# New planner constants for the head of an mLSTM and two-MLP kernel: filling matmuls, sigmoids, ranks

## The chip, the core and the metric

The kernel runs on one core of a Trainium2 chip. The metric is the device time of one execution in microseconds (us); the median of three timed runs stands for a kernel. Engines are TensorE (PE; its weight loads are PEld), VectorE (DVE), ScalarE (ACT), GpSimd (POOL) and SyncE (SP), which here only issues DMAs.

## What is computed

An mLSTM over 4 batches of 8 heads with 768 steps of dimension 40, and then two dense blocks on 3072 tokens with 320 features and 2048 hidden ones. Cut to what matters:

```python
m_new = maximum(f_gate[t] + m, i_gate[t])
f_stab, i_stab = exp(f_gate[t] + m - m_new), exp(i_gate[t] - m_new)
C = f_stab * C + i_stab * outer(v[t], k[t])
n = f_stab * n + i_stab * k[t]
y[t] = sigmoid(o_gate[t]) * (C @ q[t]) / maximum(abs(n @ q[t]), 1)
# first dense block            second dense block
h = x @ w_in                   h = x @ w_in
g = 0 | (h+1)**2/4 | h         g = maximum(h, 0)**2
x = g @ w_out                  out = g @ w_out
```

In the first dense block g is 0 for h <= -1, h for h >= 1 and the parabola between.

## The kernel before

**Tiling.** The sequence is cut into 24 chunks of 128 steps (4 batches of 6); a chunk is also a tile of 128 tokens. The order of the chunks is the first chunk of each batch, then the second of each, and so on. In this text "the first, second, third chunk" are the first chunks of batches 0, 1 and 2, and the fourth is that of batch 3.

**The gates** (`gate_part`, L380) are handled in two parts: part 0 is the first chunk of each batch, part 1 is the other five. Each runs a scan (L388), subtractions (L394 to L399), three exponentials on ACT (L405, L408, L411), some memsets and a copy on DVE (L414 to L416) and a scan (L419); the input gates are transposed by PE (L443) and copied by ACT (L447).

**Attention** (`attention`, L457) of a chunk: `spread` (L507) puts the decays of four heads on all partitions with PE, twice a chunk; `decay` (L512) is a DVE scan over them; `last` (L518) copies their last column with ACT; `scores` (L540) is PE; `weigh` (L521) multiplies the scores by the decays on DVE; `v_in`, `k_in` and `q_in` (L547, L569, L561) are POOL or DVE; `outer` (L575) makes the new state with PE, `update` (L585, L589) adds it; `read` (L612, L616) gives the output, which is normed (L626 to L631, L636) with the sigmoid `sig` (L553) of the output gate. `again` (L641) copies 64 columns. `to_xT` (L655, L665) transposes it with PE and splits it in a high and a low part, for dense products in two parts.

**Weights** (`weights`, L280). There are 16 blocks of 128 hidden features for each dense block. One comes as 64-bit floats by one DMA (L286); ACT (L290) and DVE (L298, L299, L303, L311) turn it into a 32-bit float, a copy gives the high part `w` (L272), and a subtraction the low part (L320, L324 on DVE or POOL). For the blocks listed in PLO the low part is made by PE instead (`plo`: L352, L353, in two halves, each copied out by ACT), one half after the other in the order of the block's number; these halves use the PSUM bank `acc2`.

**Dense** (`dense`, L676). Three chunks make a token block; for a token block j and a feature block f, `mm1` (L697) gives the hidden features, ACT, DVE and POOL apply the gate and split it, `mm2` (L750) adds to the output in `acc0` to `acc2`. The first three token blocks take feature blocks 0 to 7 in turn and then 8 to 15.

**What sets the order.** `Plan.order` (L58) is a list scheduler. Each step has a rank, the engines it can run on, a planned duration, and what it needs and makes. Whenever an engine is free in planned time, the ready step with the lowest rank is taken; steps that share the SBUF port of DVE and POOL exclude each other in the plan; buffers of a tag are handed out by the rank of the step that allocates. The list it gives is the order in which each engine runs its instructions on the chip, with no change at run time. Ranks are set as follows: chunk number m has a rank `at` from AT, or later from its token block's first use minus LEAD1; a weight block has WAT (first dense block), and its DMA's rank is lower by WDMA; the gates' part 1 has GATE, and its two stores to DRAM GATE + GDMA; a sigmoid has `at - 4`, plus SIGL for the first two chunks.

**Filling matmuls** (L815, L818). FILL matmuls of 128x128 by 128x160 bf16, which compute nothing that is used, have a rank behind all else, so that they go wherever PE has nothing ready in planned time. The planned duration is 0.22 for the first 30 and FDUR for the others.

```python
for i in range(FILL):
    plan.add(T, -97 if i == 0 else 1e6, 0.22 if i < 30 else FDUR, lambda i=i: idle(i == 0), ...)
...
plan.add(A, at - 4 + SIGL * (c == 0 and b < 2), act(DM), sig, [("vko", n)], [("sg", n)])
...
plan.add(Y, rank - WDMA, 2.75, load, make=[("wraw", K)])
```

Of the kernel before, what the change touches and what calls it, by code (L numbers as in the profile page):

```python
# [35 lines left out]
class Plan:  # L36
# [3 lines left out]

    TABLE = {"sig": "sigmoid", "a1": "exp", "a2": "exp", "a3": "exp"}
    LAT = {"T": 0.25, "SP": 1.9}

# [12 lines left out]
    def order(self):  # L58
        n = len(self.steps)
        maker, inst, users, alloc = {}, {}, {}, {}  # L60
        for i, (eng, rank, fn, need, make) in enumerate(self.steps):
            for key in make:
                assert key not in maker, key
                maker[key] = i
                if key[:2] not in alloc:
                    alloc[key[:2]] = i
                    inst.setdefault(key[0], []).append(key[1])
            for key in need + make:
                users.setdefault(key[:2], set()).add(i)
        deps = [set() for _ in range(n)]  # L70
        for i, (eng, rank, fn, need, make) in enumerate(self.steps):
            deps[i] |= {maker[key] for key in need}
        for tag, seq in inst.items():
            if tag not in self.bufs:
                continue
            b = self.bufs[tag]
            seq.sort(key=lambda x: self.steps[alloc[tag, x]][1])
            for k in range(1, len(seq)):
                if alloc[tag, seq[k]] != alloc[tag, seq[k - 1]]:
                    deps[alloc[tag, seq[k]]].add(alloc[tag, seq[k - 1]])  # L80
                if k >= b:
                    deps[alloc[tag, seq[k]]] |= users[tag, seq[k - b]]
        left = [len(d) for d in deps]
        after = [[] for _ in range(n)]
        for i, d in enumerate(deps):
            assert i not in d, self.steps[i]
            for j in d:
                after[j].append(i)
        ready, on = [0.0] * n, [None] * n
        free, queue = {}, {}  # L90

        def enqueue(i):
            rank, options = self.steps[i][1], self.steps[i][0]
            best = None
            for e, dur in options.items():
                q = queue.setdefault(e, [])
                ahead = sum(self.steps[k][0][e] for k in q if self.steps[k][1] <= rank)
                end = max(free.setdefault(e, 0.0) + ahead, ready[i]) + dur + (PEN if best else 0)
                if best is None or end < best[0]:
                    best = end, e  # L100
            on[i] = best[1]
            queue[best[1]].append(i)

        for i in range(n):
            if not left[i]:
                enqueue(i)
        out = []
        port, table = 0.0, None
        while len(out) < n:
            t, eng = min((max(free[e], min(ready[i] for i in q)), e) for e, q in queue.items() if q)  # L110
            i = min((i for i in queue[eng] if ready[i] <= t), key=lambda i: (self.steps[i][1], i))
            queue[eng].remove(i)
            out.append((t, i))
            dur = self.steps[i][0][eng]
            want = self.TABLE.get(self.steps[i][2].__name__)
            if want and want != table:
                table, dur = want, dur + 1.3
            shared = eng == "P" or isinstance(dur, Shared)
            free[eng] = end = (max(t, port) if shared else t) + dur
            if shared:  # L120
                port = end
            for j in after[i]:
                left[j] -= 1
                lat = 0.02 if eng in self.steps[j][0] and eng != "SP" else self.LAT.get(eng, 0.1)
                ready[j] = max(ready[j], end + lat)
                if not left[j]:
                    enqueue(j)
        self.span = max(free.values())
        return [(self.steps[i][2], on[i]) for _, i in out]
# [17 lines left out]
def act(n):  # L147
    return 0.2 + n * 0.00084
# [10 lines left out]
TURNS1 = [(0, 0, 8), (1, 0, 8), (2, 0, 8), (0, 8, 16), (1, 8, 16), (2, 8, 16)]  # L159
TURNS2 = [(6, 0, 8), (7, 0, 8), (6, 8, 16), (7, 8, 16), (8, 0, 8), (9, 0, 8), (8, 8, 16), (9, 8, 16)]  # L160
SPR = 6
AT = [-24, -19, -12, -4, 2, 2.0, 5.5, 8.5, 10.0]
WAT = [-13, -13.0, -7.5, -7.5, -3, -3.5, 1, 0.0, 6.0, 14.5, 16.0, 17.5, 16.5, 23.0, 22.5, 28.0]
LEAD1 = {3: [10.0, 11.5, 3.5], 4: [10.5, 6, 2.0], 5: [11.0, 8.0, 4.5], 6: [11.5, 7.5, 7.5], 7: [9.0, 5, 4.0]}
LEAD2 = {3: [12, 9, 3], 4: [12, 9, 6, 3]}
XTB, PAB = 3, 9
RAWB, DB = 3, 2
EARLY = 1
QB = 1
GATE = -14  # L170
FILL, FDUR = 140, 0.2
SIGL, GDMA = 3, 6
PLO = (0, 2, 3, 5, 6, 7)
WLEAD2 = (13, 0)
WDMA = 6
SGNV, LOV = (4, 4), (4, 0)
GLOV = (0, 1, 2, 3)

# [6 lines left out]
def kernel(  # L185
# [81 lines left out]
    def av(n):  # L267
        return {A: act(n), V: dve2(n)}
# [11 lines left out]
    def weights(part, f, rank):  # L280
# [46 lines left out]
        sg = P if f % 4 >= SGNV[part] else V  # L327
        plan.add(Y, rank - WDMA, 2.75, load, make=[("wraw", K)])
        plan.add(A, rank, act(WH), a_abs, [("wraw", K)], [("wt", K)])
# [8 lines left out]
        plan.add(av(WH), rank, 0, a_hi, [("wt", K, 3)], [(W, part + 1)])  # L338
        if part == 0 and f in PLO:
            plo(f, rank, z)  # L340
# [6 lines left out]
    def plo(f, rank, z):  # L347
        W, K = f"w{f}", (0, f)
        for i, (c0, c1) in enumerate(((0, WH // 2), (WH // 2, WH))):
            def sub(c0=c0, c1=c1):  # L350
                x = t_["idle_ps"][:, 0:c1 - c0]
                nc.tensor.matmul(out=x, lhsT=ident, rhs=z["t"][:, c0:c1], start=True, stop=False)  # L352
                nc.tensor.matmul(out=x, lhsT=nident, rhs=z["w"][:, c0:c1], start=False, stop=True)  # L353

            def put(c0=c0, c1=c1):
                x, w = t_["idle_ps"], z["w"]
                copy(A, w[:, WH + c0:WH + min(c1, WL)], x[:, 0:min(c1, WL) - c0])
                if c1 > WL:
                    copy(A, w[64:128, WL:c1], x[64:128, WL - c0:c1 - c0])

            key = ("acc2", -1, f, i)
            last = plan.plo
            plan.plo = key + (1,)
            plan.add(T, rank, 0.85, sub, [("wt", K, 3), (W, 1), ("acc2", -1), ("nid", 0), last], [key])
            plan.add(A, rank, act(352) + 0.2 * i, put, [key], [key + (1,), (W, 1, 1 + i)])
# [464 lines left out]
    gate_part(0, 1, -50)  # L830
    gate_part(1, NCB, GATE)
    for f in range(NF):
        weights(0, f, WAT[f])
    m = 0
    for j, (part, mine) in enumerate(blocks):
        nch = len(mine)
        for k, n in enumerate(mine):
            if part == 0:
                at = first_of[j] - LEAD1[j][k] if m >= len(AT) else AT[m]
                m += 1  # L840
# [6 lines left out]
    for f in range(NF):  # L847
        weights(1, f, max(last_of[0, f] + 1, first_use[1, f] - WLEAD2[f // 8]))
    for j, f0, f1 in visits:
# [84 lines left out]
```

## Time and profile before

| | |
|---|---|
| Median of three timed runs | 888.95 us (888.65 to 889.16) |
| The profiled execution | 887.01 us |
| its span on the core | 885.2 us |
| PE busy | 868.0 us |
| DVE busy | 468.3 us |
| ACT busy | 443.5 us |
| POOL busy | 333.1 us |

A row of the timeline gives the start and the duration in us, the engine, the line of the kernel, the operation, what it writes and reads, and how many instructions are merged in it; the bracket is the idle time of the engine just before it and what ended it. The windows give busy time of each engine in a stretch, and as PEclk the granted share of TensorE's full clock (1.00 is 2.4 GHz, 0.50 is 1.2 GHz). The ends of matmuls are modelled, so pieces of PE overlap a little.

### The profile page before, as it was taken

Reading aid. Unit: us, or ns where it says so; the run is one execution under the profiler, and the core shown is the slowest. Engines: PE = TensorE matmul, PEld = TensorE weight load, DVE = VectorE, ACT = ScalarE, POOL = GpSimd, SP = SyncE. Lnnn points to the kernel's source line nnn. Section 1 sums busy time; section 2 is a strip of 40 time slices with the busy share of each in tenths; the row PEclk is TensorE's granted clock in tenths of the full one; section 3 lists DMA queues with packets and bytes.
Section 4 is the critical chain, followed back from the end, with each engine's and each line's share of the span. In section 5 each row is a group of like instructions: output and inputs, shape, how many; then the busy total and the mean of one; then the engine's idle time right before and its main releaser. Section 6 shows DMA issues by size and latency. Waiting matters only on the chain.

```text
span 885.2 us, 14965 instructions
## 1 busy us (share of the span) xinstructions
PE 868.0 (98%) x5782; PEld 845.9 (96%) x5782; DVE 468.3 (53%) x834; ACT 443.5 (50%) x919; POOL 333.1 (38%) x318
## 2 busy tenths in 40 slices
PE   7989999999999999999999999999999999999997
PEld 6868999999999999999999999999999999999997
DVE  4788888996765655345437788822222222222221
ACT  5255457764554554545568765533343434343433
POOL 3212431003221246446335666533333333333333
PEclk6789999999999999999999999999999999999999
DMA  6555562455441434334002333011010000000000
GB/s 202 186 180 163 172 176 88 142 171 165 124 125 47 120 106 122 108 100 124 28 10 68 131 121 126 10 34 41 26 33 26 25 26 16 8 16 9 16 9 23
DMA packets 55979, 75.72 MB, mean 86 GB/s; under 512 B 7252, under 2 KB 44792, under 8 KB 55908
## 3 DMA queue, kind: packets, MB, share of 16 engines
q1 hardware_dynamic: 55908, 74.77, 27.1%
q8 instruction: 45, 0.74, 0.3%
q14 instruction: 26, 0.21, 0.1%
HBM read 65.90 MB, written 8.85 MB: 84 GB/s over the span
## 4 chain that ended last, share of the span: by engine, by line
PE 93%; DVE 3%; DMA 2%; ACT 1%; issue 0%; SPq 0%; DVEq 0%; ACTq 0%
PE h L697 39%; PE acc L750 38%; PE v L616 4%; PE s L540 3%; PE s L655 2%; PE v L612 2%; PE v L575 1%; PE s L507 1%; PE acc L352 1%; DMA vko<-in_vko_dram 1%; DVE d L512 1%; DVE wt L303 1%; DMA qk<-in_qk_dram 0%; PE acc L818 0%; PE h L507 0%
## 5 line engine op out<-in xcount | busy, mean ns | idle before, releaser
L750 PE MATMUL acc<-w,g 128*128 128x320 f32 x2304 | 379.3, 311 | 0.0
L750 PEld LDWEIGHTS acc<-w,g 128*128 128x128 f32 x2304 | 350.6, 188 | 2.5 <-DVE o L778 0.3
L697 PE MATMUL h<-xTh,w 128*128 128x384 f32 x1280 | 351.8, 340 | 0.4 <-DVE r L715 0.3
L725 POOL TENSOR_TENSOR g<-r,g 128x384 fp32r<-128x384 f32 x192 | 204.9, 1069 | 285.0 <-ACT g L272 270.1
L697 PE MATMUL h<-xTl,w 128*128 128x384 f32 x768 | 258.8, 337 | 0.0
L697 PEld LDWEIGHTS h<-xTh,w 128*128 128x128 f32 x1280 | 233.4, 188 | 1.7 <-DVE r L715 0.9
L717 DVE TENSOR_TENSOR r<-r,h 128x384 f32<-128x384 f32 x128 | 70.8, 554 | 233.4 <-ACT r L704 233.3
L272 ACT ACTIVATE g<-r 128x384 fp32r<-128x384 f32 x256 | 133.5, 523 | 114.2 <-DVE r L717 64.3
L697 PEld LDWEIGHTS h<-xTl,w 128*128 128x128 f32 x768 | 144.8, 189 | 0.0
L704 ACT ACTIVATE r<-h 128x384 f32<-128x384 f32 x128 | 62.7, 490 | 137.3 <-PE h L697 104.6
L702 ACT ACTIVATE r<-h,half 128x384 f32<-128x384 f32 x128 | 74.1, 579 | 94.1 <-PE h L697 91.6
L715 DVE SCALAR_TENSOR_TENSOR r<-r,h 128x384 f32<-128x384 f32 x128 | 70.0, 548 | 72.6 <-ACT r L708 69.4
L708 ACT ACTIVATE r<-r 128x384 f32<-128x384 f32 x128 | 67.0, 523 | 3.0
L512 DVE TENSOR_TENSOR_SCAN d<-fb,csb 128x512 f32<-128x512 f32 x36 | 50.2, 1395 | 9.5 <-PE v L616 9.4
L547 POOL TENSOR_TENSOR vt<-vko,it 128x369 f32<-128x369 f32 x24 | 23.1, 961 | 80.0 <-PE v L616 53.6
L616 PEld LDWEIGHTS v<-vt,d 128*128 128x128 f32 x384 | 49.1, 197 | 0.5
L616 PE MATMUL v<-vt,d 128*128 128x41 f32 x384 | 49.2, 279 | 0.0
L569 POOL TENSOR_TENSOR kt<-vko,ws 128x360 f32<-128x360 f32 x19 | 16.8, 885 | 75.2 <-ACT ws L518 75.2
L725 DVE TENSOR_TENSOR g<-r,g 128x384 fp32r<-128x384 f32 x64 | 37.9, 594 | 8.7 <-ACT g L272 8.3
L521 DVE TENSOR_TENSOR d<-s,d 128x512 f32<-128x512 f32 x48 | 31.5, 680 | 17.8 <-PE s L540 17.6
L561 POOL TENSOR_TENSOR qt<-qh,ab 120x384 f32<-120x384 f32 x20 | 22.2, 1110 | 35.6 <-DMA ab<-a 28.3
L595 POOL TENSOR_TENSOR C<-cx,csb 120x369 f32<-120x369 f32 x16 | 15.4, 960 | 53.3 <-DVE cx L589 50.2
(76 smaller groups left out, 686.7 us busy)
## 6 DMA issues: line engine op xcount, KB each, us to landing
wraw<-in_wts_dram SPq DMA_DIRECT2D x32, 704.0 KB
vko<-in_vko_dram SPq DMA_DIRECT2D x24, 524.5 KB
fb<-f SPq DMA_DIRECT2D x18, 512.0 KB
qk<-in_qk_dram SPq DMA_DIRECT2D x48, 160.0 KB
x<-x SPq DMA_DIRECT2D x24, 192.0 KB
x<-o SPq DMA_DIRECT2D x24, 160.0 KB
out_dram<-o SPq DMA_DIRECT2D x24, 160.0 KB
qh<-in_qh_dram SPq DMA_DIRECT2D x20, 180.0 KB
```

Of the source, the lines that this page charges most:

```text
L272: nc.scalar.activation(out=out, in_=in_, func=ACTF.Copy)
L512: nc.vector.tensor_tensor_scan(out=d.rearrange("p h t -> p (h t)"), data0=(z["fb"][a] if spr else z["fb"][:, 4 * a:4 * a + 4]).rearrange(" ...
L521: nc.vector.tensor_mul(out=z["d", a], in0=z["s", a], in1=z["d", a])
L616: nc.tensor.matmul(out=z["y"][:, E * h:E * (h + 1)], lhsT=z["d", a][:, h - 4 * a], rhs=z["vt"][:, h], start=(h == 0 and c == 0), stop=True ...
L697: nc.tensor.matmul(out=h, lhsT=a, rhs=b, start=(i == 0), stop=(i == 7))
L702: nc.scalar.activation(out=r, in_=z["h"], func=ACTF.Relu, scale=0.5, bias=half)
L704: nc.scalar.activation(out=r, in_=z["h"], func=ACTF.Relu)
L708: nc.scalar.activation(out=z["r"], in_=z["r"], func=ACTF.Square)
L715: nc.vector.scalar_tensor_tensor(out=r, in0=r, scalar=1.0, in1=z["h"], op0=ALU.min, op1=ALU.max)
L717: nc.vector.tensor_mul(out=r, in0=r, in1=z["h"])
L725: engine[e].tensor_sub(out=z["g1"], in0=z["r"], in1=z["g0"].bitcast(F32))
L750: nc.tensor.matmul(out=acc[k][:, 0:DM], lhsT=a, rhs=b, start=(f == f0 and i == 0), stop=(f == f1 - 1 and i == 2))
```

## The change

All constants below feed the planner; the steps and their instructions stay as they are, except that the low parts of feature blocks 1 and 4 of the first dense block are made by PE and ACT instead of DVE or POOL. There are 170 filling matmuls instead of 140, with a planned duration of 0.135 instead of 0.2 for those behind the thirtieth. Steps of PE that start before 5 us of planned time are planned at twice their duration. The two first sigmoids have ranks higher by 6. The ranks of chunks and weights, the gates' part 1, its stores and the weight DMAs are set anew.

```diff
+    COLD = 5.0
     TABLE = {"sig": "sigmoid", "a1": "exp", "a2": "exp", "a3": "exp"}
...
+            if eng == "T" and t < self.COLD:
+                dur *= 2
...
-AT = [-24, -19, -12, -4, 2, 2.0, 5.5, 8.5, 10.0]
-WAT = [-13, -13.0, -7.5, -7.5, -3, -3.5, 1, 0.0, 6.0, 14.5, 16.0, 17.5, 16.5, 23.0, 22.5, 28.0]
-LEAD1 = {3: [10.0, 11.5, 3.5], 4: [10.5, 6, 2.0], 5: [11.0, 8.0, 4.5], 6: [11.5, 7.5, 7.5], 7: [9.0, 5, 4.0]}
+AT = [-24, -19, -13, -4, 1.5, 2.0, 5.5, 8.5, 13.0]
+WAT = [-13, -10.0, -7.5, -7.5, -3, -6.5, 1, 0.0, 12.0, 15.0, 17.5, 17.5, 15.5, 22.0, 22.5, 25.5]
+LEAD1 = {3: [11.0, 12.0, 3.0], 4: [12.5, 8, 2.0], 5: [9.0, 5.0, 2.5], 6: [14.5, 10.5, 10.5], 7: [9.5, 5.5, 4.5]}
...
-GATE = -14
-FILL, FDUR = 140, 0.2
-SIGL, GDMA = 3, 6
-PLO = (0, 2, 3, 5, 6, 7)
-WLEAD2 = (13, 0)
-WDMA = 6
+GATE = -13
+FILL, FDUR = 170, 0.135
+SIGL = 9
+GDMA = 13
+PLO = (0, 1, 2, 3, 4, 5, 6, 7)
+WLEAD2 = (13, -1)
+WDMA = 7
```

## Rows read from the trace of the kernel before

**Rows 1.** The page, busy us of each engine, share of the span, instructions.
```profile
PE 868.0 (98%) x5782; PEld 845.9 (96%) x5782; DVE 468.3 (53%) x834; ACT 443.5 (50%) x919; POOL 333.1 (38%) x318
```

**Rows 2.** Windows: start:end, length, busy of PE, PEld, DVE, ACT, POOL; PEclk, DMA, GB/s.
```profile
30.00:35.00 5.00, 5.00 (x38) 4.46 (x37) 2.76 (x7) 0.00 (x0) 2.23 (x3) 0.50 0.08 25
35.00:40.00 5.00, 4.73 (x35) 3.86 (x33) 4.97 (x8) 2.44 (x6) 1.00 (x1) 1.00 0.75 247
40.00:45.00 5.00, 3.10 (x36) 2.79 (x34) 4.83 (x12) 2.26 (x4) 1.66 (x2) 1.00 0.77 259
45.00:50.00 5.00, 4.96 (x24) 4.06 (x24) 4.54 (x7) 2.97 (x6) 0.38 (x1) 0.52 0.29 82
...
60.00:70.00 10.00, 8.71 (x56) 6.86 (x57) 9.83 (x15) 7.50 (x18) 0.79 (x1) 1.00 0.42 147
...
80.00:90.00 10.00, 10.00 (x62) 8.18 (x61) 8.42 (x19) 4.70 (x12) 3.73 (x4) 0.86 0.65 213
```

**Rows 3.** Timeline of PE, 13 to 67 us.
```profile
13.07 0.72 PE L818 MATMUL acc<-x 128*128 128x160 bf16 x4
...
17.98 2.32 PE L818 MATMUL acc<-x 128*128 128x160 bf16 x16
21.17 2.04 PE L507 MATMUL s<-w,csb 36*128 36x128 f32 x8 [0.88 <-DVE d L521]
...
32.61 2.53 PE L818 MATMUL acc<-x 128*128 128x160 bf16 x18
35.41 0.53 PE L655 MATMUL s<-csb,xn 128*128 128x128 f32 x3 [0.27 <-DVE xn L636]
...
50.77 1.75 PE L540 MATMUL s<-qk 40*128 40x128 f32 x16
...
66.55 0.44 PE L697 MATMUL h<-xTh,w 128*128 128x384 f32 x1
```

**Rows 4.** Timeline of DVE, 19 to 65 us.
```profile
19.39 0.59 DVE L415 MEMSET w<- 36x640 f32 x1
20.02 0.42 DVE L416 COPY w<-w 36x5 f32<-36x5 f32 x1
...
43.10 0.29 DVE L320 TENSOR_TENSOR w<-wt,w 64x128 fp32r<-64x128 f32 x1
43.40 1.18 DVE L324 TENSOR_TENSOR w<-wt,w 128x576 fp32r<-128x576 f32 x1
...
48.01 1.22 DVE L512 TENSOR_TENSOR_SCAN d<-s,csb 128x512 f32<-128x512 f32 x1 [0.43 <-PE s L507]
...
52.55 1.29 DVE L521 TENSOR_TENSOR d<-s,d 128x512 f32<-128x512 f32 x2 [2.07 <-PE s L540]
...
61.97 0.51 DVE L298 TENSOR_SCALAR wt<-wt 128x704 f32<-128x704 f32 x1
62.51 0.53 DVE L299 TENSOR_SCALAR wt<-wt 128x704 int32<-128x704 int32 x1
...
64.19 0.53 DVE L665 TENSOR_TENSOR xTl<-s,xTh 128x384 fp32r<-128x384 f32 x1
```

**Rows 5.** Timeline of ACT, 8 to 18 us.
```profile
8.15 1.28 ACT L553 ACT_TABLE_LOAD   x1
10.46 0.47 ACT L553 ACTIVATE sg<-vko 128x320 f32<-128x320 f32 x1 [1.02 <-DMA vko<-in_vko_dram]
...
17.09 0.21 ACT L518 ACTIVATE ws<-d 128x4 f32<-128x4 f32 x1 [0.27 <-DVE d L512]
```

**Rows 6.** Timeline of PE, one half of a low part at full clock.
```profile
56.84 0.80 PE L352 MATMUL acc<-wt,csb 128*128 128x352 f32 x2
57.20 0.59 PE L353 MATMUL acc<-w,nident 128*128 128x352 f32 x1
57.63 0.31 PE L818 MATMUL acc<-x 128*128 128x160 bf16 x2
```

**Rows 7.** Waits of PE behind 66 us: us in total, times, longest.
```profile
PE v L612 <- DVE cx L589: 1.4, 2, 1.0
```

## The prediction

> **What bounds the kernel now.** I read the busy shares first: TensorE (PE) is busy for 98% of the span [rows 1], and every window behind 130 us shows it full. The page's shares hide the head, so the next view is the table by windows [rows 2]. There the reader sees three things. PE is "busy" in 30:35 at half clock (1.2 GHz), and what it does is partly filling matmuls that compute nothing. In 40:45 it is busy for only 3.10 of 5 us, and in 45:50 the clock is back at half. And VectorE (DVE), which is busy for only 2.76 of 5 us in 30:35, is full from 35 us on (4.83 of 5, then 9.83 of 10 in 60:70). The timeline of PE [rows 3] gives the date that counts: the first dense matmul (L697, feature block 0 of token block 0) starts at 66.55 us. From there on PE hardly waits any more; the largest wait listed is 1.4 us in two pieces [rows 7]. So the end is that date plus PE work that the change hardly touches: **a microsecond off the head is a microsecond off the kernel**, as long as PE stays full behind it.
>
> What holds 66.55? The first dense matmul needs three chunks through attention and transposed; the last step of that is the low half of the third chunk's transpose on DVE, at 64.19 us [rows 4]. Going back from it on DVE from 64 to 35 us nothing is idle but two waits, both for PE: 0.43 us before a decay scan (L512) and 2.07 us before the third chunk's weighing (L521) [rows 4]. So the head is, from 35 us on, DVE's work plus 2.50 us. Before 35 us it is PE at half clock: spreads (L507) of 2.04 us each, outer products, reads, scores, one behind the other [rows 3].
>
> **How the planner's edits become an order.** All ranks, FILL, FDUR and COLD only feed a list scheduler; on the chip each engine runs its queue in that fixed order. I use its planned times for one thing, who stands before whom and how many fills go into a gap (planned gap divided by the planned length of a fill); no duration is taken from it.
>
> **Fills.** A fill at half clock takes 2.32/16 = 0.145 us [rows 3]. FDUR goes from 0.2 to 0.135, near the cold one, so a planned gap gets half as many again. COLD doubles the first ones' planned length up to 5 us of planned time: 19 instead of 30 stand before the first transpose. PE waits there for the gates anyway, so that costs nothing. Along the cold stretch:
> - before the first spread 4 fills become 6: 2 x 0.145 = +0.29. PE waits for nothing there, so this is on the path.
> - before the first spread of the second chunk there are 16, a planned gap of 3.2 us, and PE then still waits 0.88 us for DVE [rows 3]. DVE is late there because the memset and copy of the later gates (0.59 and 0.42) stand before the weighing [rows 4]. In the changed plan the second chunk's sigmoid no longer holds ACT, the first chunk's `last` copies are planned 1.3 us earlier, and the weighing is picked first. The planned gap falls to 2.4 us, so 18 fills. DVE releases about 1.0 us earlier, but 18 x 0.145 = 2.6 us of fills behind a spread that ends 0.3 later let PE go at about 20.9 instead of 21.17: -0.27.
> - before the reads 2 become 4: +0.29, together with the two above about +0.0 when I count the first only through the second.
> - behind the second chunk's scores 18 become about 26. If the clock rises as it did near 35 us (0.50 granted in 30:35, 1.00 in 35:40 [rows 2]), they end near 35.9, and the transpose that now starts at 35.41 [rows 3] comes 0.5 later. I cost it at nothing, because DVE has its weight work to do there; without that cover it is +0.5.
>
> **The sigmoids.** SIGL moves the first two chunks' sigmoids to ranks -19 and -14. By the planner's own due times the first does not move: when ScalarE comes free at 6.87 planned, its load is due at 7.10 and the later exponentials only at 7.38, so it is still taken first, with its table load [rows 5]. The second goes behind the third chunk's, because the `sg` buffers are handed out by rank. That frees ACT near 15 us, where the trace shows `last` at 17.09 waiting 0.27 for DVE and not for ACT [rows 5]: nothing by itself. What is queued behind the third chunk's sigmoid, which now has to wait for its load, are weight steps due much later.
> The Trainium skill ("ScalarE: Activation LUTs", section Table sets) asks to do all of one set before switching, and puts a switch at about 2.66 us. Here a table load shows 1.28 us [rows 5], and the count of loads does not fall by my reading. If it fell by one on the path, an estimate by that page would be 886.3 for this edit alone.
>
> **Weights.** PLO adds feature blocks 1 and 4 to those whose low parts PE and ACT make. This takes 0.29 + 1.18 = 1.47 us off DVE at 43 us, right before the second chunk's output [rows 4]: -1.47 on the path. It adds two halves each on PE; a half takes 57.63 - 56.84 = 0.79 at full clock [rows 6]. Block 1's are made before 66 us, where PE has fills and waits to spare: 0. Block 4's fall next to the dense start or behind it: 2 x 0.79 = +1.58. ACT gets two copies for each, and is free for more than half of 40:45 [rows 2].
>
> **The third chunk, one rank earlier.** AT[2] from -12 to -13 changes one thing of weight. Both its spreads now get their PSUM buffer before the second chunk's transpose; before, they tied, and the second spread stood behind it, at half clock, with the decay that waited 0.43 us and the scores that ran at 50.77 and held DVE 2.07 us [rows 3, 4]. Both waits should go: -2.50. What is late next is DVE itself. Block 7's first weight step (0.51 + 0.53, planned into a hole of the third chunk's chain) should fall behind that chain: -1.04 by its two rows [rows 4]. Bounds of these three together: -1.47, if the holes only move, to about -7, if blocks 4 and 5 fall behind as well (they are some 2 to 3 us of DVE each at the same prices).
>
> **The rest** (GDMA, WDMA, WLEAD2, LEAD1, later AT and WAT). SP issues the later gates' decays for the DMA chunks later and weights one rank earlier; in the head its queue has time between issues. Behind 66 us PE waits little [rows 7], so there is little to win: I take 0, with -1.4 (that wait gone) to +1.5 as bounds. A dip of the clock shows in 80:90 (0.86 granted) [rows 2]; it costs 1.4 us there (0.14 x 10) and may stay, move or go: 0, with +-1.4.
>
> **Sum:** 0.0 - 2.50 - 1.47 - 1.04 + 1.58 = -3.43 us. The profiled execution took 887.01 us with a span of 885.2; it would become 883.6. The median of the timed runs is 888.95, 1.94 above the profiled one, and the sum stands for it as well: 888.95 - 3.43 = **885.5**. By its bounds alone this case holds 883.5 to 887.1.
>
> **Rivals.**
> 1. *The clock rises near 21 us instead of 35.* For: the 18 fills before 35 us were followed by full clock, the 16 at 18 us were not, and these become 18. Against: two fills are little, and a spread follows. PE's cold work from 21.17 to the end of the second scores at 32.6 would halve, 5.7 us at most; DVE, idle for 2.24 us in 30:35 [rows 2], takes over as the bound. I take 3.5 more: 882.0.
> 2. *The first sigmoid does go behind the exponentials.* ACT copies the input gates (which free a PSUM buffer for the scores) right behind it; the sigmoid waited 1.02 us for its load and began at 10.46 [rows 5]. Without it some 2 us of the first chunk go: 883.5. My hand count of due times speaks against it.
> 3. *DVE bounds the stretch behind the dense start too.* It is busy 9.83 of 10 us in 60:70 [rows 2]; what falls behind the start must still be done, and PE waits for it there. Then only DVE's saved 1.47 counts, and PE's added halves (up to 3.2 us) are on the path: 887.2 to 890.7, no change.
> 4. *Slower: fills on the path.* The cold stretch gets some 15 more fills, 15 x 0.145 = 2.2 us; PE's waits there are 0.88 and 0.27 us [rows 3]. If the clock does not rise, they delay the second chunk, and DVE then stands idle where I count it full. It decides from the point where the fills before 35.41 end over 1.15 us later than now; with the gain of the third chunk eaten by it: 891.2.
>
> **Chances.** Forecast 0.42, rival 1 0.18, rival 2 0.04, rival 3 0.17, rival 4 0.19. What a measurement can tell from no change is 0.2%, 1.8 us: faster 0.64, same 0.17, slower 0.19. The range reaches from rival 1 with its bound to rival 4: 880.0 to 891.5.
>
> **What would show it.** The first L697 near 62.5 us; no wait of over 1 us on DVE before the third chunk's L521; six groups of eight L507 before the second L655, five now; L352 x32 and L353 x16 instead of 24 and 12, with L320 and L324 two fewer. I am wrong if the first L697 stays within 1 us of 66.55, or if it comes early and waits of PE for DVE or ACT between it and 120 us add up to over 2 us.

## The result and the profile after

The changed kernel takes **893.59 us** (median of 20 executions, 888.09 to 907.92) where the kernel before takes 887.57 beside it (883.00 to 891.09): a ratio of **1.0059, 95% interval 1.0036 to 1.0082**. It is slower, by some 5 us; the forecast was 885.5, with 891.5 as the end of its range. Some executions run over 1.5% longer than the fastest of the same kernel (903.36 and 907.92 here); the ratios leave them out, and one run below (e12b) has no trace to read, because its profiled execution was of that kind. The profiled execution took 893.85 us with a span of 892.1, 6.9 more than the span of before. In the changed kernel most lines are four further down: L697 is L701, L507 L511, L818 L822, L272 L276, L298 L302, L616 L620, L655 L659, L665 L669.

The page of the changed kernel first, its busy times (us, share, instructions), the answer to [rows 1]:

```profile
PE 876.2 (98%) x5824; PEld 854.0 (96%) x5824; DVE 467.2 (52%) x828; ACT 444.7 (50%) x925; POOL 335.1 (38%) x320
```

PE is busy 8.2 us longer, DVE only 1.1 less. Then the windows of the changed kernel, with the columns of [rows 2], and one more, 70:80:

```profile
35.00:40.00 5.00, 5.00 (x36) 4.56 (x34) 3.53 (x5) 1.10 (x4) 0.00 (x0) 0.94 0.94 241
40.00:45.00 5.00, 5.00 (x23) 3.98 (x23) 2.81 (x7) 0.86 (x2) 3.27 (x4) 0.50 0.57 179
45.00:50.00 5.00, 3.71 (x33) 3.04 (x32) 3.06 (x7) 2.51 (x6) 0.00 (x0) 0.87 0.44 145
...
70.00:80.00 10.00, 10.00 (x62) 9.14 (x61) 7.93 (x15) 4.10 (x9) 1.48 (x2) 0.85 0.49 159
80.00:90.00 10.00, 10.00 (x42) 7.82 (x40) 5.48 (x11) 4.12 (x12) 2.45 (x3) 0.64 0.21 59
```

Two things differ from [rows 2]. DVE, which was full from 35 us on (4.97, 4.83, 4.54 of 5), has 3.53, 2.81 and 3.06: it no longer bounds this stretch. And the clock is at half in 40:45, where it was full, and lower in 80:90 (0.64 against 0.86). The window 70:80 of the kernel before, for comparison:

```profile
70.00:80.00 10.00, 10.00 (x80) 9.04 (x77) 9.12 (x17) 4.67 (x11) 2.13 (x2) 0.97 0.54 166
```

The timeline of PE in the changed kernel, the answer to [rows 3]:

```profile
17.66 2.58 PE L822 MATMUL acc<-x 128*128 128x160 bf16 x18
20.17 2.08 PE L511 MATMUL s<-w,csb 36*128 36x128 f32 x8
...
31.77 3.38 PE L822 MATMUL acc<-x 128*128 128x160 bf16 x24
...
36.15 0.49 PE L659 MATMUL s<-csb,xn 128*128 128x128 f32 x3
...
38.73 1.46 PE L511 MATMUL s<-w,csb 36*128 36x128 f32 x8
40.12 1.93 PE L620 MATMUL v<-vt,d 128*128 128x41 f32 x8
...
48.29 0.52 PE L659 MATMUL s<-csb,xn 128*128 128x128 f32 x3
...
60.33 0.51 PE L822 MATMUL acc<-x 128*128 128x160 bf16 x5 [1.57 <-ACT w L276]
...
66.03 0.44 PE L701 MATMUL h<-xTh,w 128*128 128x384 f32 x1
...
100.96 1.49 PE L822 MATMUL acc<-x 128*128 128x160 bf16 x19
```

**The dense start is at 66.03 instead of 66.55**; the forecast had it near 62.5. So the head gave 0.5 us and the rest of the span (892.1 - 66.03 = 826.07 against 818.65) took 7.4. New are 19 fills at 100.96, behind the start (before, no fill came behind it), and the length of a wait: the fill at 60.33 waits 1.57 us for ACT, where the longest such wait before was 0.7. (A spread of 2.08 us at 20.17 and fills of 3.38/24 = 0.141 us show half clock up to 35 us.)

DVE's longer waits in the changed kernel, the answer to the two in [rows 4]:

```profile
42.09 0.17 DVE L630 TENSOR_SCALAR rc<-v 128x8 f32<-128x8 f32 x1 [2.25 <-PE v L620]
...
49.37 0.56 DVE L669 TENSOR_TENSOR xTl<-s,xTh 128x384 fp32r<-128x384 f32 x1 [1.91 <-ACT xTh L276]
...
51.89 1.28 DVE L525 TENSOR_TENSOR d<-s,d 128x512 f32<-128x512 f32 x2
...
59.14 0.53 DVE L302 TENSOR_SCALAR wt<-wt 128x704 f32<-128x704 f32 x1 [1.83 <-ACT wt L294]
...
60.15 0.48 DVE L640 TENSOR_TENSOR xn<-v,sg 128x320 f32<-128x320 f32 x1
...
63.16 0.56 DVE L669 TENSOR_TENSOR xTl<-s,xTh 128x384 fp32r<-128x384 f32 x1 [0.81 <-ACT xTh L276]
```

The two waits of before are gone (L525 at 51.89 follows without one), but 2.25 + 1.91 + 1.83 + 0.81 = 6.80 us stand in place of 2.50, and two shorter ones (0.93 and 0.31, at 36 and 37 us) ahead of them. The 1.83 is followed back on ACT and on SP's queue, here in the changed kernel:

```profile
58.27 0.84 ACT L294 ACTIVATE wt<-wraw 128x704 f32<-128x704 f32 x1 [1.44 <-DMA wraw<-in_wts_dram]
...
59.81 0.46 ACT L276 ACTIVATE w<-acc 128x352 fp32r<-128x352 f32 x1
```
```profile
51.43 1.62 SPq L470 DMA_DIRECT2D qk<-in_qk_dram  x2
53.15 9.61 SPq L290 DMA_DIRECT2D wraw<-in_wts_dram  x4
```

and SP's queue in the kernel before:

```profile
41.62 6.35 SPq L286 DMA_DIRECT2D wraw<-in_wts_dram  x2
...
52.58 1.62 SPq L466 DMA_DIRECT2D qk<-in_qk_dram  x2
```

Before, the loads of two weight blocks (4 and 5) stand ahead of the `qk` load of the fifth chunk. In the changed order they stand behind it, and this `qk` load waits for the third chunk's scores to free its buffer: **the first weight load goes out at 53.15 instead of 41.62**, the second right behind it (before, at 47.65). ACT's L294 waits for the data, DVE's L302 for ACT, the third chunk's norm (L640) stands behind L302, and ACT's copy of a half (59.81) stands behind L294, so that PE's fill waits at 60.33 for the bank `acc2`.

### The profile page after: what moved, and what is told of

Its sections match the earlier page's. It is cut to its first block, busy times and chain, and to the rows that moved or that the text cites. A ratio compares the mean times of both kernels' runs of the same rounds, so it can differ in the third digit from the quotient of the medians.

```text
span 892.1 us, 15056 instructions
## 1 busy us (share of the span) xinstructions
PE 876.2 (98%) x5824; PEld 854.0 (96%) x5824; DVE 467.2 (52%) x828; ACT 444.7 (50%) x925; POOL 335.1 (38%) x320
## 4 chain that ended last, share of the span: by engine, by line
PE 94%; DVE 2%; DMA 2%; ACT 1%; issue 0%; POOL 0%; DVEq 0%; ACTq 0%
PE h L701 39%; PE acc L754 38%; PE v L620 4%; PE s L544 3%; PE s L659 2%; PE s L511 2%; PE v L579 2%; PE acc L822 1%; PE v L616 1%; PE acc L356 1%; DMA fb<-f 1%; DVE d L516 1%; DMA wraw<-in_wts_dram 1%; PE h L511 0%; DMA w<-in_gates_dram 0%
## 5 line engine op out<-in xcount | busy, mean ns | idle before, releaser
L701 PE MATMUL h<-xTh,w 128*128 128x384 f32 x1280 | 352.4, 340 | 0.5 <-DVE r L719 0.3
L701 PE MATMUL h<-xTl,w 128*128 128x384 f32 x768 | 258.8, 337 | 0.0
L701 PEld LDWEIGHTS h<-xTh,w 128*128 128x128 f32 x1280 | 233.5, 188 | 2.8 <-DVE r L719 1.6
L276 ACT ACTIVATE g<-r 128x384 fp32r<-128x384 f32 x256 | 133.8, 523 | 109.4 <-DVE r L721 65.5
L701 PEld LDWEIGHTS h<-xTl,w 128*128 128x128 f32 x768 | 144.7, 188 | 0.0
L620 PEld LDWEIGHTS v<-vt,d 128*128 128x128 f32 x384 | 50.1, 201 | 1.3 <-DVE d L525 0.2
L620 PE MATMUL v<-vt,d 128*128 128x41 f32 x384 | 50.9, 284 | 0.0
L573 POOL TENSOR_TENSOR kt<-vko,ws 128x360 f32<-128x360 f32 x20 | 16.9, 847 | 89.7 <-ACT ws L522 83.5
L729 DVE TENSOR_TENSOR g<-r,g 128x384 fp32r<-128x384 f32 x64 | 40.7, 637 | 6.4 <-ACT g L276 6.2
L525 DVE TENSOR_TENSOR d<-s,d 128x512 f32<-128x512 f32 x48 | 31.2, 678 | 9.8 <-PE s L544 9.8
```

The lines of the kernel that those rows point to most:

```text
L276: nc.scalar.activation(out=out, in_=in_, func=ACTF.Copy)
L525: nc.vector.tensor_mul(out=z["d", a], in0=z["s", a], in1=z["d", a])
L620: nc.tensor.matmul(out=z["y"][:, E * h:E * (h + 1)], lhsT=z["d", a][:, h - 4 * a], rhs=z["vt"][:, h], start=(h == 0 and c == 0), stop=True ...
L701: nc.tensor.matmul(out=h, lhsT=a, rhs=b, start=(i == 0), stop=(i == 7))
L729: engine[e].tensor_sub(out=z["g1"], in0=z["r"], in1=z["g0"].bitcast(F32))
```

## The theories

**A**: the edits of the ranks do shorten the third chunk, as predicted, but the order as a whole puts new waits into the head (halves over one PSUM bank, loads on SP) and new work behind the dense start (halves, fills). **B**: the clock decides; it rises and falls at other places, and the edits matter only through it. **C**: one edit is to blame and the others are sound.

In the table "start" is the first dense matmul and "rest" the span behind it, both of the profiled execution; "half clock" is the time at half clock behind the start, from windows of 1 us (2 x (1 - PEclk), summed; the last 15 us of the span, where PE runs out of work, are left out). "Held" means that the order of the kernel named (e16: of after, e7: of before) was kept and only the named steps were taken out, moved or added; the others were planned anew.

| | median us | ratio to before, 95% | start | rest | half clock |
|---|---|---|---|---|---|
| before | 887.57 | 1 | 66.55 | 818.65 | 3.4 |
| after | 893.59 | 1.0059 (1.0036 to 1.0082) | 66.03 | 826.07 | 10.2 |
| e9 before, ranks alone | 887.46 | 0.9991 (0.996 to 1.0022) | 62.89 | 818.31 | 6.8 |
| e11 before, fills alone | 888.89 | 0.9991 (0.9958 to 1.0024) | 62.05 | 828.75 | 23.9 |
| e12b before, sigmoids alone | 889.09 | 1.002 (0.9987 to 1.0054) | - | - | - |
| e8 before, PLO of 1 and 4 | 895.42 | 1.0088 (1.0057 to 1.0119) | 72.10 | 824.10 | 10.3 |
| e13 before, PLO of 1 | 897.50 | 1.0085 (1.0054 to 1.0116) | 71.54 | 824.06 | 13.6 |
| e14 before, PLO of 4 | 889.78 | 1.0036 (1.0004 to 1.0068) | 67.36 | 820.34 | 2.4 |
| e10 after, PLO as before | 903.92 | 1.0153 (1.0116 to 1.0191) | 71.78 | 830.62 | 20.5 |
| e1 after, late fills out, held | 890.20 | 1.0034 (1.0002 to 1.0066) | 59.59 | 825.51 | 10.2 |
| e2 e1, fills among spreads, held | 892.41 | 1.0051 (1.0026 to 1.0075) | 60.93 | 829.77 | 13.7 |
| e3 after, low parts on DVE, held | 892.50 | 1.0028 (0.9996 to 1.006) | 68.25 | 823.55 | 10.2 |
| e15 after, qk load behind, held | 890.20 | 1.0017 (0.9986 to 1.0048) | 65.28 | 824.72 | 10.2 |
| e16 e15 and e1, held | 889.50 | 1.0019 (0.9992 to 1.0046) | 61.88 | 825.42 | 10.2 |
| e12a after, 8 more fills, held | 890.42 | 1.0039 (1.001 to 1.0068) | 62.93 | 825.47 | 10.2 |
| e5 before, gap at 41 us filled, held | 886.62 | 0.9974 (0.9948 to 0.9999) | 64.72 | 820.88 | 6.8 |
| e6 before, 10 more fills at 18 us, held | 886.14 | 0.9977 (0.9946 to 1.0009) | 67.95 | 816.65 | 0.0 |
| e7 both, held | 890.29 | 1.0015 (0.9982 to 1.0049) | 67.19 | 825.31 | 16.9 |

The ratio is to executions of the kernel before that ran beside each kernel, so the medians of two rows are not compared with each other. The column "start" and the ratio don't always agree: of one order the executions differ by several us (below), and one is profiled.

## One edit alone

**Ranks** (e9): AT, WAT, LEAD1, GATE, GDMA, WLEAD2 and WDMA of the change in the kernel before.

> The kernel before with the changed ranks alone (AT, WAT, LEAD1, GATE, GDMA, WLEAD2, WDMA; fills, sigmoids and PLO as before). The reasoning of the prediction: the third chunk's two waits of DVE go, the start comes 2.5 to 3.5 us earlier, the rest stays, and the time falls by as much. Theory PE work: attention's small matmuls of the chunks 4 to 6 come in a row behind the start, the half-clock stretch there grows from 3.4 to about 10 us, the rest grows by about 3.4 us, and the time stays or rises by up to 3 us.

The start and DVE's only waits between 35 us and it, in e9:

```profile
39.09 1.22 DVE L512 TENSOR_TENSOR_SCAN d<-s,csb 128x512 f32<-128x512 f32 x1 [0.75 <-PE s L507]
...
59.90 0.56 DVE L665 TENSOR_TENSOR xTl<-s,xTh 128x384 fp32r<-128x384 f32 x1 [0.63 <-ACT xTh L272]
```
```profile
62.89 0.34 PE L697 MATMUL h<-xTh,w 128*128 128x384 f32 x1
```

The start is where it was forecast: waits of 1.38 us instead of 2.50, a start at 62.89, and a profiled span 4.0 shorter. But two other things differ in this execution. It is 0.8 us ahead at the second chunk's first spread already (20.39 against 21.17). And its clock is full from 35 us to the start, where the kernel before shows 0.52 in 45:50 [rows 2] and 0.80 in 50:55. e5 below keeps the order of the kernel before and has a full clock from 40 us on, and there DVE's only wait is this:

```profile
50.60 1.29 DVE L521 TENSOR_TENSOR d<-s,d 128x512 f32<-128x512 f32 x2 [0.72 <-PE s L540]
```

So 1.8 of the 2.50 us were not due to the order but to half clock. Counted from the first transpose, the start comes after 31.14 us in the kernel before, 29.80 in e5 and 28.26 in e9: some 1.5 us are left for the ranks. And the median says no change: the profiled execution of e9 (882.97) is the fastest of its twelve. So the gain of the ranks isn't shown in the time.

**Fills** (e11: FILL, FDUR, COLD) and **sigmoids** (e12b: SIGL 9 for 3):

> The kernel before with FILL 170, FDUR 0.135 and COLD alone; the planner sets its order anew. Theory clock: 16 fills at 18 us become some 24, the clock rises near 20 us in part of the executions, and those start the dense work 3 to 6 us earlier; median 1 to 3 us below the kernel before, with a wider spread. Theory fills on the path (rival 4 of the prediction): about 15 more fills before 35 us delay the second chunk by 1 to 2 us: 889.5 to 890.

> The kernel before with SIGL 9 alone; the planner sets its order anew. By the prediction: the first sigmoid stays where it is, the second moves behind the third; DVE weighs the first chunk about 1 us earlier and PE waits less before 21.17 us; from 35 us DVE is the bound: within 1 us of the kernel before. Rival 2: the first sigmoid goes behind the exponentials and the scores start near 9 us: 2 us less.

Neither can be told from no change. In the profiled execution of e11 the clock rose early (the spread at 20.90 takes 1.48 us) and the start is at 62.05, but 23.9 us at half clock behind it take that back.

**Low parts by PE** (e8, e13, e14), and the change without them (e10):

```diff
-PLO = (0, 2, 3, 5, 6, 7)
+PLO = (0, 1, 2, 3, 4, 5, 6, 7)    e8;  e13: (0, 1, 2, 3, 5, 6, 7);  e14: (0, 2, 3, 4, 5, 6, 7)
```

> The kernel before with one constant changed: the low parts of feature blocks 1 and 4 of the first dense block by PE and ACT too (the planner sets its order anew). Theory PE work: the four more halves shift as much PE work behind the dense start; the first dense matmul comes up to 1.5 us earlier, the rest grows by about 3.2 us, and the time rises by 1.5 to 3.2 us. The reasoning of the prediction (blocks 1 hidden, 1.47 us off DVE in the head, 1.58 on PE): no change, within 0.5 us.

> The kernel before with only feature block 1 added to PLO; the planner sets its order anew. Theory ring: it is block 1, whose halves stand on PE before the second chunk's transpose near 45 us and wait there for ACT's copies, behind a weight step of ACT that waits for its DMA; the start of the dense work moves 3 to 5 us later, and the time rises by 3 to 6 us, most of what both blocks cost. Theory PE work: two halves of 0.79 us more: 1.6 us. By the prediction: 1.47 us less.

> The kernel before with feature block 4 alone added to PLO. Theory A (a block's cost is that of halves made ahead of the dense start, one by one over a PSUM bank and an ACT copy, and block 4's fall behind it): first L697 stays within 1 us of 66.5, the time rises by about 2 x 0.79 = 1.6 us, ratio 1.002. Rival (any seventh block makes the ring of halves and copies the bound of the head): first L697 near 71 as with block 1, ratio 1.008.

> The changed kernel with PLO as before, (0, 2, 3, 5, 6, 7), and all else changed; the planner sets its order anew. Theory ring: the halves of a low part pass through one PSUM bank in a ring of PE, ACT and PE, and PE, whose queue is in order, waits in them for ACT (4.3 us in PLO alone, which made the kernel before 0.9% slower); without blocks 1 and 4 the loss goes, and ranks and fills are left: 883 to 888, a ratio to the kernel before of 0.995 to 1.000. Theory clock alone: the loss of the change is the half-clock stretch behind the start and the fills there, which stay: 890 to 894.

Block 1 alone costs what both cost. e13's trace shows why, on ACT, on PE, on DVE, and in the windows of 5 us:

```profile
42.48 0.85 ACT L290 ACTIVATE wt<-wraw 128x704 f32<-128x704 f32 x1 [0.99 <-DMA wraw<-in_wts_dram]
43.35 0.46 ACT L272 ACTIVATE w<-acc 128x352 fp32r<-128x352 f32 x1
```
```profile
43.87 0.37 PE L818 MATMUL acc<-x 128*128 128x160 bf16 x3 [1.75 <-ACT w L272]
...
47.08 0.84 PE L655 MATMUL s<-csb,xn 128*128 128x128 f32 x3
...
53.59 2.08 PE L540 MATMUL s<-qk 40*128 40x128 f32 x16
...
71.54 0.44 PE L697 MATMUL h<-xTh,w 128*128 128x384 f32 x1
```
```profile
50.10 1.22 DVE L512 TENSOR_TENSOR_SCAN d<-s,csb 128x512 f32<-128x512 f32 x1 [1.72 <-PE s L507]
...
55.70 1.29 DVE L521 TENSOR_TENSOR d<-s,d 128x512 f32<-128x512 f32 x2 [3.13 <-PE s L540]
```
```profile
45.00:50.00 5.00, 4.26 (x25) 3.57 (x22) 2.99 (x5) 3.15 (x7) 0.00 (x0) 0.54 0.44 148
50.00:55.00 5.00, 4.45 (x25) 3.22 (x26) 2.47 (x3) 1.35 (x3) 1.51 (x1) 0.50 0.14 24
```

A half leaves `acc2` by an ACT copy, and the fills write the same bank. ACT's copy at 43.35 stands behind a weight step that waits for its DMA; PE's fill waits 1.75 for that copy, and everything behind it on PE waits too. The clock then is at half from 45 to 55, the third chunk's scores take 2.08 us (1.75 in the kernel before, 1.16 at full clock), and DVE waits 1.72 and 3.13 where it waited 0.43 and 2.07. Of the 10.4 us more span, 5.0 are in the start; the other 5.4 lie behind it, where 10.2 us more are at half clock. Block 4's halves are made later: its start is 67.36, 0.8 later than before, and the ratio is 1.0036. **So in the order of the kernel before the dear one is block 1, which the forecast had at nothing.** Theory C falls all the same: the change without the two blocks (e10) is slower still, 1.0153. Its order has the weight loads late too (53.43), a fill that waits 3.35 for ACT, and 20.5 us of half clock behind the start. A list planned anew is another list everywhere, and here the edits' effects don't add.

## Steps taken out of the changed order

**Late fills** (e1: those numbered 150 and up, which are the 20 behind the start; e2: as e1, with five fills behind each spread of the second chunks of batches 0 and 1 instead):

```diff
+        if i >= 150:
+            return
```

> The changed kernel with its order held; only the last 20 filling matmuls (one at 88.6 us, 19 at 100.96 us, all behind the dense start) are left out. Theory PE: behind the first dense matmul PE is full, and what it has to do there sets the end; the 19 fills took 1.49 us, so the time falls by 1.3 to 1.5 us against the changed kernel (893.6), to about 892.2. Theory DVE: behind the start PE only waits for DVE and ACT in other places, so the time stays at 893.6 and a wait of PE of about 1.3 us shows where the fills were.

> The changed kernel with its order held; the same 20 fills are not left out but put into the stretch between 73 and 80 us, five behind each of the four spreads of the fifth and sixth chunk, where attention's small matmuls run one behind the other and the clock falls to half from 77.0 to 87.1 us. Theory clock: the fills keep it at full, PE does the work of 10.1 us in about 5, so the time falls by 3.5 to 5 us against the changed kernel, to 889 to 890. Theory PE work alone (the clock falls whatever is put there, or PE waits for DVE in this stretch): the time stays within 0.5 us of the changed kernel, and PEclk still shows half between 77 and 87 us.

Without them the ratio falls from 1.0059 to 1.0034; by their rows they take 1.49/19 = 0.078 each, 1.6 us for 20, on a PE that is full. The intervals overlap, and e12a below, which adds eight fills and takes nothing out, stands at 1.0039: the ratio shows no gain, and the size rests on the rows. Moved among the spreads they brought nothing that can be told (1.0051): 13.7 us of half clock behind the start against 10.2.

**Low parts of 1 and 4 back on DVE** (e3), at the place of ACT's second copy:

> The changed kernel with its order held, but the low parts of feature blocks 1 and 4 are made by DVE again, at the place in the order where ACT copied them out. Theory PE work: of the 16 halves 9 run behind the dense start, against 4 of 12 before; at 0.79 us each the halves of block 4, and of the others that its absence lets pass earlier, give 1.6 to 4 us back: 889.6 to 892. Theory DVE: DVE's 2 us more delay the start by as much, and the time stays or rises to 895.

The start goes to 68.25 and the rest falls by 2.5: DVE's work is back in the head, and the halves behind the start go from 9 to 7. The time, 1.0028, is not told apart from either kernel.

**The qk load behind the two weight loads** (e15; e16 leaves out the late fills too):

```diff
+        i = [k for k, x in enumerate(seq) if x[0].__name__ == "ld_qk"][4]
+        k = [k for k, x in enumerate(seq) if x[0].__name__ == "load" and k > i][1]
+        seq.insert(k, seq.pop(i))
```

> The changed kernel with one DMA moved on SP: the fifth chunk's qk load goes behind the next two weight loads, where the kernel before has it. All else keeps its place. Theory A (the weight loads stand behind a qk load that waits for the third chunk's scores, and ACT, DVE and the third chunk's norm wait for them): the two loads are issued near 45 us instead of 53.15, ACT's L294 at 58 us no longer waits 1.44 for its DMA, DVE's L302 no longer 1.83 for ACT, PE's fill no longer 1.57; the first L701 moves from 66.03 to about 64.2, and the time by -1.5 to -2.0, to a ratio near 1.004. Rival (PE's order and the clock set the third chunk, the load only ends a wait that another would end next): the waits go, first L701 stays within 0.5 us of 66.03, ratio stays near 1.006.

> The changed kernel with the same DMA moved and the fills numbered 150 and up left out (they are the twenty behind the dense start). If both are costs by themselves and add up: the ratio of the kernel without those fills, 1.0034, less 0.2%: about 1.0015, and still not faster than the kernel before, because the four added halves behind the start (4 x 0.79 = 3.2 us) are still there. Rival (effects do not add): 1.003 or more.

e15 on SP and on DVE, and its windows:

```profile
49.01 3.59 SPq L290 DMA_DIRECT2D wraw<-in_wts_dram  x2
52.69 1.62 SPq L470 DMA_DIRECT2D qk<-in_qk_dram  x2
```
```profile
56.41 0.53 DVE L302 TENSOR_SCALAR wt<-wt 128x704 f32<-128x704 f32 x1 [0.79 <-ACT wt L294]
...
62.41 0.56 DVE L669 TENSOR_TENSOR xTl<-s,xTh 128x384 fp32r<-128x384 f32 x1 [2.78 <-ACT xTh L276]
```
```profile
45.00:50.00 5.00, 4.61 (x38) 4.28 (x37) 3.98 (x7) 2.33 (x5) 0.00 (x0) 0.66 0.37 112
...
55.00:60.00 5.00, 3.89 (x22) 2.90 (x22) 3.77 (x6) 2.95 (x7) 1.21 (x1) 0.66 0.70 224
```

and e16, which has the same order up to the start, with its first two transposes:

```profile
45.00:50.00 5.00, 4.93 (x54) 4.26 (x53) 4.80 (x10) 2.32 (x5) 0.00 (x0) 1.00 0.53 145
```
```profile
35.67 0.49 PE L659 MATMUL s<-csb,xn 128*128 128x128 f32 x3
...
45.17 0.52 PE L659 MATMUL s<-csb,xn 128*128 128x128 f32 x3
```

The one moved DMA brings the first load out 4.1 us earlier (I expected 8; they now wait for their own buffers), the wait of 1.83 falls to 0.79, that of PE's fill from 1.57 to 0.55, and the ratio from 1.0059 to 1.0017. In its profiled execution the clock is at half for part of 45:50 and 55:60, and a wait of 2.78 comes up, so its start is only 0.75 earlier. In e16 the clock holds from 36 us on (1.00 in every window of 5 us from 40 to 60), and the start is 61.88. That the loads are a cost is shown by the waits; the ratio of e15 is no longer told apart from 1, but its interval overlaps that of the changed kernel. Both removals together (1.0019) bring no more than this one.

## The clock

e5, e6 and e7 double fills of the kernel before in their places, e12a those of the changed kernel ahead of 20 us:

```diff
+        for _ in range(2 if 100 <= i < 112 else 1):    e5;  e6: 46 <= i < 56;  e7: both;  e12a, after: 36 <= i < 44
```

> The kernel before with its order held; the last 12 fills of the 26 at 41 us are doubled, so that the gap up to the second transpose at 45.0 us is filled to about 44.0. Theory clock: the clock does not fall at 45 us, the spread there takes 1.15 instead of 2.07 us and what follows up to 52 us runs at full clock, so the two waits of DVE (0.43 and 2.07 us) shrink and the time falls by 1.5 to 2.5 us against the kernel before. Theory DVE: DVE is full from 35 us on and takes the time by itself; within 0.5 us of the kernel before.

> The kernel before with its order held; 10 of the 16 fills at 18 us are doubled, 26 in all. In two executions of the changed kernel's head (18 fills there) the clock rose near 20 us and the first dense matmul came at 59.6 and 60.9 us, in a third it did not and came at 66.0. Theory clock: with 26 fills the clock rises near 21 us in nearly every execution; the fills cost up to 0.6 us beyond PE's wait of 0.88 there, the cold work up to 33 us halves, the first dense matmul comes 3 to 6 us earlier than 66.55, what follows stays at 818 to 820 us, and the time falls by 3 to 5 us against the kernel before. Theory DVE: DVE is the bound of the head in any case; the start moves by less than 1 us and the time rises by up to 0.6 us.

> The kernel before with its order held; 10 of the 16 fills at 18 us and the last 12 of the 26 at 41 us doubled. Theory clock: the gains of the two gaps add up as far as DVE does not take over as the bound: 4 to 7 us below the kernel before. Theory DVE: no more than the second gap alone gave, 0.997 of the kernel before.

> The changed kernel with the fills 36 to 43 doubled, which stand before the second chunk's first spread near 18 us: 26 fills there instead of 18. If it is the length of uninterrupted PE work there that lets the clock rise near 20 us, the spreads at 20 and 23 us take about 1.2 instead of 2.08 and the first L701 comes near 60 to 62, ratio 1.001 or less. Rival (whether it rises there varies from one execution to the next): the times of its executions spread as widely as those of the changed kernel (several us), with the median within 0.2% of it plus the 8 x 0.145 = 1.2 us that the added fills take at half clock, ratio 1.006 to 1.008.

With the gap at 41 us filled (38 fills instead of 26) the window 45:50 shows 1.00 in e5 and in e7, against 0.52 in [rows 2] and 0.61 in e6, which leaves that gap. e5's start is 64.72, and its ratio, 0.9974, is the lowest here; but e6, which leaves that gap, has 0.9977, and e7, which fills it too, 1.0015. That the filled gap saves time is not shown. In its profiled execution e5 gains 1.8 us at the start and loses 2.2 behind it, with 6.8 us at half clock there instead of 3.4.

Ahead of 20 us it is different. e12a and e1 on PE:

```profile
18.84 3.65 PE L823 MATMUL acc<-x 128*128 128x160 bf16 x26
22.42 1.22 PE L511 MATMUL s<-w,csb 36*128 36x128 f32 x8
```
```profile
16.99 2.58 PE L824 MATMUL acc<-x 128*128 128x160 bf16 x18
19.50 1.32 PE L511 MATMUL s<-w,csb 36*128 36x128 f32 x8
```

In both the spread behind the fills runs at full clock but for its first part (1.16 is the whole at full clock). In the changed kernel, in e15 and in e16 it takes 2.08 us behind the same 18 fills; in e6 it takes 2.08 behind 26. After, e1, e2 and e12a agree in their order up to the start but for the eight fills of e12a, and start at 66.03, 59.59, 60.93 and 62.93. So rival 1 is real: **the same order starts up to 6.4 us earlier or later** (0.7 of it is there already at that spread). What decides it stays open; more fills ahead of it didn't settle it. Whether the edit makes it likelier is open too: the clock rose near 20 us in four of the nine profiled executions with the changed fills (e1, e2, e11, e12a) and in none of the eight read with those of the kernel before, two of which had 26 there (e6, e7).

The second place in the head where the clock differs is between the first two transposes (L659). In the changed order they stand 12.14 us apart (36.15 and 48.29), with the clock at half from 39 to 46 us, and so they do in e1, e2 and e12a (12.19 to 12.20, with a stretch at half clock too). In e15 and e16, whose order is the same up to there, the clock holds up to 45 us, and they stand 9.89 and 9.50 apart. From the second transpose to the start it is 17.74 us in the changed kernel and 17.76 in e1, and 16.71 in e16, whose weight loads go out earlier. Taken together, 2.6 us of half clock and 1.0 us of late loads would bring the start of the changed kernel from 66.03 to 62.4, where it was forecast. These are single executions, but they tell the two causes apart: theory B holds for the larger part of what is missing in the head, theory A for the loads.

The Trainium skill ("TensorE: Matmul & The Clock Gate", Part 1) says that the number of cold matmuls differs from run to run and that the ramp costs less than 1% of a typical span. The traces agree: behind the same 18 fills the spread is at half clock in one execution and not in another, and their starts are 6.4 us apart, 0.7% of 892 us. But that is as much as the whole change.

## Why the prediction was wrong

Where the 6.9 us of span come from, by the profiled executions:

| term | forecast | found |
|---|---|---|
| dense start | near -4 | -0.5 |
| halves behind the start | +1.58 (2 of them) | +3.95 (9 instead of 4, at 0.79) |
| fills behind the start | not seen | +1.6 |
| half clock behind the start | 0, +-1.4 | +3.4 (half of 10.2 - 3.4) |
| PE's waits behind the start | 0 | -0.6 (1.6 instead of 2.2) |
| sum | -3.4 by its own terms | +7.9; 1.0 more than the 6.9, unexplained |

The prediction's first sign of being wrong came: the start stayed within 1 us of 66.55. Two sums in it are loose by themselves. Its three terms for the head give -5.0, a start at 61.5; "near 62.5" needs a half of block 4 ahead of it. And its own bounds don't end at 887.1: -1.47 with the +1.58 of the halves is no gain at all (889.1).

**What was right.** The order: six spreads before the second transpose, 16 halves, 6, 18 and 4 fills where these numbers were given and 24 for "about 26"; the first sigmoid stays and the second goes behind the third. The cold stretch: the first spread of the second chunk at 20.17, even 0.7 earlier than forecast. The two waits of the third chunk do go, and block 7's first weight step (1.04 us) falls behind the third chunk's chain. Nor did rival 4 come: the fills before the first transpose end at 35.15, as before (35.14), and not 1.15 later. And DVE didn't take over behind the start, as rival 3 had it (7.93 and 5.48 of 10 us in 70:80 and 80:90); but its other half came, the added halves on PE's path.

**"Block 1's are made before 66 us, where PE has fills and waits to spare: 0", and with it +1.58 for block 4's two halves.** This step failed. Block 1's halves do come before the start. But the halves follow one another in the order of the block's number, PE, ACT, PE over one bank, and the head has room for seven of them (eight before). So block 1's take the room of others, and five more fall behind the start instead of two: +3.95 instead of +1.58. I counted PE's time for a half and not its way. In 35 to 66 us PE's fills wait 4.0 us for ACT's copies in the changed kernel and waited 1.6 before; these are the groups of waits of the one and of the other (total, times, longest):

```profile
PE acc L822 <- ACT w L276: 4.0, 5, 1.6
```
```profile
PE acc L818 <- ACT w L272: 1.6, 3, 0.7
```

Alone, in the order of the kernel before, the edit costs 0.85%, with the wait of 1.75 us first and half clock behind it. In the changed order these waits don't hold the head: e16 has 3.2 us of them and starts at 61.88. What the edit took off DVE was no gain where DVE waited for PE and ACT instead.

**"Both waits should go: -2.50."** They went, but the term was mis-sized. I took both from an execution with half clock in 45:50 and put them down to the order. At full clock the same order waits 0.72 (e5).

**"In the head [SP's] queue has time between issues."** This step failed too. I looked at the time between issues and not at what the next one in the queue waits for. The changed plan as a whole puts the load that depends on the third chunk ahead of two weight loads; the ranks alone don't (in e9 these go out at 44.46 and 49.45, ahead of that load at 49.87). On the chip the third chunk's scores came no earlier than 50.20 (47.08 in e16, where the clock held), and the weight loads had to wait. That is the 1.83 on DVE and the 1.57 on PE, and some 1.0 us of the start.

**"What is late next is DVE itself."** It wasn't: the moved spread (38.73) and the reads behind it (40.12) run at half clock, 1.46 and 1.93 us, and DVE waits 2.25 for them (1.11 in e16, at full clock). I had asked what the spreads no longer hold up, and not what they now hold up, and I let the clock between 35 us and the start stand as it was.

**Behind the start** I counted two halves where five more lie there, no fills where 20 do, and let the clock stand. The added halves and fills lie there because the order puts them there. The half clock is less sure: the order of the kernel before shows 0.0, 3.4, 6.8 and 16.9 us of it behind the start in four executions (e6, before, e5, e7), the changed one 10.2 in six of seven. "A microsecond off the head is a microsecond off the kernel" held within one order: after and e12a start at 66.03 and 62.93, and the rest is 826.07 and 825.47; e1, without the 1.6 us of fills, has 59.59 and 825.51. It doesn't hold from one order to another, because the work that an order takes out of the head is left for later.

How much of the 0.59% is due to each can't be said: single steps taken out give 0.25 to 0.42 points less, eight fills put in (e12a) 0.20 less, all with intervals of +-0.3. The terms above are read from single executions; as causes of the time they are argued and not shown.

## What to carry to other kernels

Where a planner writes the queues, read the changed queue of every engine, SP's too, for an instruction that waits with others behind it: a step planned earlier can drag along the load that depends on it, past loads that were free to go. Price a wait at full clock: a wait behind work at half clock isn't the order's. Work given to an engine with idle time costs its whole way, the copies and the shared bank with the engines' own order, and not its busy time. And when executions of one order differ by more than the gain sought, a single profile shows mechanisms, and two profiles are compared stretch by stretch with the clock beside them; only many executions show the gain.

## What the runs showed of the hardware

Between executions of nearly the same instruction order the clock rose near 20 us or near 35 us, and the dense start moved by up to 6.4 us with it.

A pause of PE near 41 us was followed by half clock in 45:50 (0.52), and the same pause filled with 38 matmuls was not (1.00). But the clock fell without a pause as well: in the changed kernel near 39 us, where PE shows 5.00 of 5 us busy in 35:40 and in 40:45 with spreads and reads (0.94 and 0.50 granted). In e15 and e16 it held through the same instructions (1.00 in 40:45).

Half clock behind the dense start, between 0 and 23.9 us in these kernels, is nearly the whole difference between executions of one order: take half of it off the rest, and before, e5, e6 and e7, whose rests lie 8.7 us apart, agree within 0.9 (816.95, 817.48, 816.65, 816.86). The changed kernel comes to 820.97: 4.0 us of its rest are the order's and 3.4 the clock's.
